# A Fourier mixing layer, a dense Mish layer and their gate: a second-level product more in the dense stage, and y preloaded into PSUM in the last one

## The chip, the cores and the metric

The kernel runs on one core of a Trainium2 chip. The metric is device time in microseconds of one execution of the whole program. Its engines are TensorE (PE: matmuls; PEld: its weight loads), VectorE (DVE), ScalarE (ACT) and GpSimd (POOL); SyncE (SP) issues nearly all DMAs, in one queue. Everything is float32; a matmul takes its operands as `float32r`.

## The reference

```python
x = A_x                                            # 2048 x 640
g = sigmoid((x * gate_w).sum(-1, keepdims=True))
a = einsum("bsd,ed->bse", x, dft_hid_re)
b = einsum("bsd,ed->bse", x, dft_hid_im)
y = einsum("ts,bse->bte", dft_seq_re, a) - einsum("ts,bse->bte", dft_seq_im, b)
h = einsum("bsd,df->bsf", x, w1) + b1              # 640 -> 1728
act = h * tanh(softplus(h))                        # Mish
out = g * y + (1 - g) * einsum("bsf,fd->bsd", act, w2)
```

S = 2048 rows, D = 640 columns, F = 1728 features (13 blocks of 128 and one of 64).

## The kernel before, in words

**Numbers.** Every operand is split in two parts, h (a rounded copy, by ScalarE) and l (the rest, by VectorE): `split`, L127. One product of 128 x 128 by 128 x 512 is `mm3`: three matmuls, high by high, high by low, low by high. A bank of PSUM holds 128 x 512 sums; there are eight, handed out in turn by `psum.get` and `psum.put`.

**Stages.** There are four, one after the other on PE: the transform along the sequence (`seq`, first stored as u), the transform along the hidden axis (`hid`, gives y, stored in `ysc[d][t]`, d for a block of 128 columns, t for a tile of 512 rows), the dense first stage (640 to 1728, with Mish, stored in `asc[f][t]`), and the last stage (`out`, 1728 to 640, with the gate). Each uses the seven-product scheme of Strassen and Winograd over halves: a product of 2 x 2 halves in seven products, with sums of operands ahead and of results behind. The odd fifth block of the 640 columns (the tail) goes along as plain products.

**The dense first stage.** x transposed is the moving operand (`xt[t, k]`, k a block of 128 columns). A pair (fp, tp) takes the features fp and fp + 6 and the tiles t1 = 2 tp and t2 = 2 tp + 1; halves of the columns are blocks 0, 1 and 2, 3. Steps of a pair in `dense_first`: p5 (moving s1), d (the tail d2 for feature fp + 6, a bank of its own), p6 (s2), p3 (s4, with the tail d1), p7 (s3), p2 (a12, the second product A12 B21, with the tail d1), p4 (a22, with the tail d2). The first product, A11 B11, is not there: `dense_quads` (L829) makes it for two features and both tp at once by the seven-product scheme at a second level, in seven steps (a12, a11, s1, s2, s4, s3, a22) of nine matmuls each, for three pairs of features, with banks a and b. Its results go to DRAM (`qout`) and come back as a seed, a copy into the bank a in which the pair's p6, p7 and p4 add on. `dense_rest` computes the last 192 features in steps of 15 and 10 matmuls per tile. `ORDER` puts steps of `dense_rest` (r) and `dense_quads` (q) in turn.

**The last stage.** `ou[0]` computes tiles 0 and 1, `ou[1]` tiles 2 and 3. Order of steps: the first product of `ou[0]` in part, that of `ou[1]`, the rest of the former, then `second` and `third` of each. `second` begins with a `rest` step: the last 192 features for tile t2, in the banks e, e, p4, p4, d2, five matmuls in each. For tiles 2 and 3 act is already multiplied by q = 1 - g (QX in `out_act`, `act_q` for the last 192 features) and y by g (`gate_y`), so they add. For tiles 0 and 1 the results are multiplied by q at the end (`done`, `give`) and the gated y is added (`add_y`).

**Order.** Each engine works its instructions in the order in which the program issues them. The planner runs through the steps; at step i it issues, in this order: operand loads and operand splits (`prep`) of steps up to LEAD or LEAD_D ahead; the step's matmuls; stores that are due; the step's `post` (copies and additions out of its banks); events put there by `at(i, fn)`; then pieces of background jobs (splitting weights, sums of operands, gating of y), for as long as its count of VectorE's time is behind its count of PE's by SLACK, SLACK_D or SLACK_UP, but not in `quiet` steps. `takes`, `spare` and `SPARE` hold back free tiles for later steps. Jobs run in the order of the list `jobs`, not before step `first`.

Of the kernel before, what the change touches and what calls it, by code (L numbers as in the profile page):

```python
# [22 lines left out]
WARM, EARLY = 8, 3  # L23
LEAD = 7
LEAD_D, AHEAD_D = 6, 4
AHEAD = 9
SPARE, SPARE_D, SPARE_OUT = 3, 5, 4
SLACK, SLACK_UP, SLACK_D, QUIET = -1.0, 2.5, 1.0, 2
NR, NFS, NFX, NW, NL = 9, 22, 4, 26, 4
MM = 0.2267  # L30
BACK, NB = 16, 3
NLOAD = 6
QUIET_M, D_END = -1, 24
ORDER, Q_LEAD = "rrqrrqrqrqrqrq", 3
P_LOAD, P_SEED = 8, -1
YG_FIRST, NO_LOAD = 40, 3
XS_FIRST, XS_EACH = 160, 10
R0, R1 = (2, 4), (2, 4)
# [16 lines left out]
def fnet_mish_gate(ctx: ExitStack, tc: tile.TileContext, xn, xt, c_re, c_im, wd_re, wd_im,  # L55
# [28 lines left out]
    def tt(o, a, b, op):  # L84
        clock["dve"] += 0.14 + 0.54 * a.shape[-1] / N
        nc.vector.tensor_tensor(o, a, b, op=op)  # L86
# [4 lines left out]
    def split(h, l, src):  # L91

        copy(h, src)
        tt(l, src, f32(h), OP.subtract)

# [110 lines left out]
    def low(st, k, g, f):  # L206
# [13 lines left out]
        split(*part(st.XA[k], 3 * P, 5 * P), t[:, B2])  # L220
        split(*part(st.XT13[k], 4 * P, 5 * P), t[:, :P])
        split(*t2_part(st, k), t[:, P:2 * P])
# [83 lines left out]
    def add_out(name, f, keep=False):  # L306

        for ps, a in zip(PS[name], f):
            tt(a, ps, a, OP.add)
        if not keep:  # L310
            free_banks(name)
        return f
# [13 lines left out]
    class Problem:  # L326
# [49 lines left out]
        def second(self):  # L376
# [25 lines left out]
            def plus_y(f, d, t):  # L402
                y = YT.pop((d, t))
                tt(f, f, y, OP.add)
                FS.put(y)

            def post(p, k):
# [13 lines left out]
                elif p == "s2":  # L421
                    KEEP["u2"] = add_out("a", ys(t1, 2, 3), True) if self.early else copy_out("a", True)
# [14 lines left out]
            if st.kind == "out":  # L437
# [5 lines left out]
                rest(t2, [("e", 2, True), ("e", 3, True), ("p4", 0, True), ("p4", 1, True), ("d2", 4, True)], e_post)  # L443
            for p, k in in_turn(kh, ("22", "21", "s2", "s1"), ("22", "21", "s2", "s1"), ("22", "21", "s2", "s1")):
# [18 lines left out]
                if k == kh - 1:  # L463
                    takes[i] = (p == "21" or p == "s1" and 2) if self.early else 1 if p == "21" else 2
# [119 lines left out]

        def y_load(self, i, t, *ds):
# [49 lines left out]
    WA, W1, W2C, T2B, QW, extra = [None] * FP, [None] * (FC + 1), {}, [None] * 2, [None] * (FP // 2), []  # L635
# [8 lines left out]
    def quad_job(g, l, m):  # L644
# [3 lines left out]
        WA[2 * g], WA[2 * g + 1], QW[g] = W.get(), W.get(), W.get()  # L648
        split(*WA[2 * g], l)
        split(*WA[2 * g + 1], m)  # L650
        yield 1
        lo, hi = slice(0, P), slice(P, 2 * P)
        for o, u, v in ((0, m[:, lo], l[:, lo]), (1, m[:, hi], m[:, lo]), (2, m[:, hi], t[:, lo]),
                        (3, l[:, hi], t[:, 2 * P:3 * P])):
            tt(t[:, o * P:o * P + P], u, v, OP.subtract)
        FX.put(l, m)
        yield 1
        split(*part(QW[g], 0, 4 * P), t)
        FS.put(t)

    def w1_job(f, ga, gb):
        t = FS.get()
        a, b, c = WA[f], W.get(), W.get()
        if f % KD == 0:
            T2B[f // KD] = W.get()
# [8 lines left out]
        split(*part(b, 0, 2 * P), t[:, B2])  # L674
        split(*part(c, 0, 2 * P), ga[:, A2])
        yield 1
        split(*part(c, 2 * P, 4 * P), gb[:, A2])
        split(*part(c, 4 * P, 5 * P), t[:, :P])
        split(*part(T2B[f // KD], f % KD * P, f % KD * P + P), t[:, P:2 * P])
        FS.put(t)  # L680
        FX.put(ga, gb)
        W1[f] = (a, b, c)
# [23 lines left out]

    def dense_jobs():
        for _ in range(NL):
            jobs.append(Job("lend", simple(lend), w=1))
        def quad(g):  # L710
            jobs.append(Job(("quad", g), lambda l, m: quad_job(g, l, m),
                            lambda: [fx_load(w1a[2 * g + i]) for i in range(2)], 3, 2, 1))
        quad(0)
        jobs.append(Job("w1c", simple(w1c_job), lambda: [fx_load(w1a[FC - 1])], 1, 1))
        jobs.append(Job("w1r", simple(w1r_job), lambda: [fx_load(w1b, KD * FR)], 1, 1))
        quad(1)
        quad(2)
        for f in range(FP):
            jobs.append(Job(("w1", f), lambda a, b, f=f: w1_job(f, a, b),
                            lambda f=f: [fx_load(w1a[f]), fx_load(w1a[f + FP])], 2 + (f % KD == 0), 2))  # L720

    def x_split(key, f):
        r = X[key] = R.get()
        split(r[0], r[1], f)
        FS.put(f)
# [8 lines left out]
    def dense_rest(t, keep, lead, end=False):  # L734
# [9 lines left out]
        def prep(lo, hi):  # L744
            for k in range(lo, hi):
                x_split(keys[k], RAW.pop(("xt", t, k)))
# [6 lines left out]
        def post_c():  # L753
# [3 lines left out]
            store(asc[FC - 1][t], a, a)  # L757
# [8 lines left out]
        def post_r():  # L766
# [7 lines left out]
            def then():  # L774
                nc.scalar.activation(a[q], a[q], AF.Mish)
                store(asc[FC][t], a[q], a)
            at(clock["step"] + 1, then)
            if not keep:
                x_free(*keys)
            else:  # L780
                x_free(*[(names[0], k, t // 2) for k in range(2)])
            if end:
                for w in W1[FC - 1:]:
# [4 lines left out]
        def wait():  # L788
            for key in ("mish", "w1c", "w1r"):
                need(key)  # L790
        step(raw, [wait], mms_c, post_c)
# [7 lines left out]
    XQ = {"a11": xt[0, 0], "a12": xt[0, 1], "a22": xt[2, 1]}  # L799
    XQ.update({o: dr.tile([P, N], F32, name=f"q{o}") for o in ("s1", "s2", "s3", "s4")})  # L800
    XD = {(tp, k, o): dr.tile([P, N], F32, name=f"x{o}_{tp}_{k}") for tp in range(2) for k in range(2) for o in XQ if o[0] == "s"}
    narrow_loads = []
# [495 lines left out]
```

## Time and profile before

| | us |
|---|---|
| three runs | 861.49, 861.83, 862.65 |
| median | 861.83 |
| profiled execution: span, first to last instruction | 860.5 |
| PE busy (3766 matmuls) | 856.2 |
| DVE busy (1281 instructions) | 732.6 |
| ACT busy (903) | 485.6 |
| DMA moved | 233.15 MB, 271 GB/s on the mean |

The page of the profile gives busy times for the whole span; the view by stretches gives them for parts of it, with the clock granted to PE and the share of time in which the DMA engines were busy. The timeline gives instructions one by one: start, length, engine, line, operation, out<-in, count, and in brackets the idle time before it and what ended it. A matmul's 0.39 us overlaps with the next, so the distance from one start to the next is its price. Since all matmuls stand on line 98 and most of DVE's work on line 86, steps are told apart by their place in the order.

### The profile page before, as it was taken

Reading aid. Unit: us, or ns where it says so; the run is one execution under the profiler, and the core shown is the slowest. Engines: PE = TensorE matmul, PEld = TensorE weight load, DVE = VectorE, ACT = ScalarE, POOL = GpSimd, SP = SyncE. Lnnn points to the kernel's source line nnn. Section 1 sums busy time; section 2 is a strip of 40 time slices with the busy share of each in tenths; the row PEclk is TensorE's granted clock in tenths of the full one; section 3 lists DMA queues with packets and bytes.
Section 4 is the critical chain, followed back from the end, with each engine's and each line's share of the span. In section 5 each row is a group of like instructions: output and inputs, shape, how many; then the busy total and the mean of one; then the engine's idle time right before and its main releaser. Section 6 shows DMA issues by size and latency. Waiting matters only on the chain.

```text
span 860.5 us, 12305 instructions
## 1 busy us (share of the span) xinstructions
PE 856.2 (100%) x3766; PEld 708.4 (82%) x3766; DVE 732.6 (85%) x1281; ACT 485.6 (56%) x903; POOL 0.2 (0%) x4
## 2 busy tenths in 40 slices
PE   9999999999999999999999999999999999999998
PEld 8888888888888888888888888888888888888886
DVE  6999988889879789998998897886578979898993
ACT  6756646464555545657656657764646756542442
POOL 0000000000000000000000000000000000000000
PEclk9999999999999999999999999999999999999999
DMA  9975758885768899898676968879998789485952
GB/s 348 345 255 198 252 164 309 281 287 198 255 234 287 280 343 363 274 316 287 207 261 242 319 197 309 287 231 370 357 377 308 230 283 315 152 289 178 353 185 110
DMA packets 126978, 233.15 MB, mean 271 GB/s; under 512 B 14656, under 2 KB 17216, under 8 KB 126912
## 3 DMA queue, kind: packets, MB, share of 16 engines
q1 hardware_dynamic: 126480, 231.72, 77.9%
q8 instruction: 29, 0.48, 0.2%
q10 hardware_dynamic: 432, 0.66, 0.2%
q14 instruction: 37, 0.30, 0.1%
HBM read 180.13 MB, written 52.18 MB: 270 GB/s over the span
## 4 chain that ended last, share of the span: by engine, by line
PE 100%; ACT 0%; issue 0%
PE ps L98 100%; ACT f L89 0%
## 5 line engine op out<-in xcount | busy, mean ns | idle before, releaser
L98 PE MATMUL ps<-rh,wh 128*128 128x512 f32 (+1 forms) x1062 | 412.1, 389 | 0.0
L98 PE MATMUL ps<-rh,wl 128*128 128x512 f32 x1046 | 405.9, 389 | 0.0
L98 PE MATMUL ps<-rl,wh 128*128 128x512 f32 x1045 | 405.9, 389 | 0.0
L89 ACT ACTIVATE rh<-f 128x512 fp32r<-128x512 f32 x419 | 250.8, 626 | 182.7 <-DVE f L86 101.7
L86 DVE TENSOR_TENSOR rl<-f,rh 128x512 fp32r<-128x512 f32 x417 | 272.5, 686 | 41.3 <-ACT rh L89 40.1
L98 PEld LDWEIGHTS ps<-rh,wh 128*128 128x128 f32 x1062 | 199.5, 188 | 41.6 <-DVE f L86 0.3
L98 PEld LDWEIGHTS ps<-rl,wh 128*128 128x128 f32 x1045 | 196.6, 188 | 40.9
L98 PEld LDWEIGHTS ps<-rh,wl 128*128 128x128 f32 x1046 | 196.3, 188 | 40.7
L86 DVE TENSOR_TENSOR f<-f,f 128x512 f32<-128x512 f32 x305 | 208.4, 688 | 9.6 <-DMA f<-act 2.2
L89 ACT ACTIVATE f<-ps 128x512 f32<-128x512 f32 (+1 forms) x145 | 83.2, 596 | 75.2 <-PE ps L98 66.7
L89 ACT ACTIVATE wh<-f 128x512 fp32r<-128x512 f32 (+3 forms) x173 | 76.7, 484 | 46.7 <-DVE f L86 36.5
L86 DVE TENSOR_TENSOR wl<-f,wh 128x512 fp32r<-128x512 f32 (+3 forms) x172 | 82.3, 512 | 20.5 <-ACT wh L89 20.4
L86 DVE TENSOR_TENSOR f<-ps,f 128x512 f32<-128x512 f32 x100 | 65.5, 683 | 16.9 <-PE ps L98 16.7
L98 PE MATMUL ps<-wh,wh 128*128 128x512 f32 x205 | 79.8, 389 | 0.0
L98 PE MATMUL ps<-wl,wh 128*128 128x512 f32 x200 | 77.8, 389 | 0.0
L98 PE MATMUL ps<-wh,wl 128*128 128x512 f32 x199 | 77.4, 389 | 0.0
L98 PEld LDWEIGHTS ps<-wh,wh 128*128 128x128 f32 x205 | 38.5, 188 | 8.2 <-ACT f L89 0.2
L98 PEld LDWEIGHTS ps<-wl,wh 128*128 128x128 f32 x200 | 37.5, 188 | 7.8
L98 PEld LDWEIGHTS ps<-wh,wl 128*128 128x128 f32 x199 | 37.4, 188 | 7.7
L732 ACT ACTIVATE f<-f,b1s 128x512 f32<-128x512 f32 x36 | 25.5, 721 | 31.5 <-DVE f L86 31.5
L86 DVE TENSOR_TENSOR wl<-fx,wh 128x640 fp32r<-128x640 f32 (+3 forms) x50 | 33.7, 680 | 5.9 <-ACT wh L89 5.9
L89 ACT ACTIVATE wh<-fx 128x640 fp32r<-128x640 f32 (+4 forms) x51 | 31.1, 615 | 5.9 <-DMA fx<-in_xn_dram 3.5
(36 smaller groups left out, 176.5 us busy)
## 6 DMA issues: line engine op xcount, KB each, us to landing
f<-in_c_re_dram SPq DMA_DIRECT2D x128, 256.0 KB, 4.0
f<-in_c_im_dram SPq DMA_DIRECT2D x128, 256.0 KB, 4.5
f<-act SPq DMA_DIRECT2D x87, 256.0 KB, 4.9
f<-u SPq DMA_DIRECT2D x80, 256.0 KB, 5.0
act<-f SPq DMA_DIRECT2D x54, 256.0 KB, 5.1
f<-in_xt_dram SPq DMA_DIRECT2D x49, 256.0 KB, 4.6
u<-f SPq DMA_DIRECT2D x40, 256.0 KB, 3.1
y<-f SPq DMA_DIRECT2D x40, 256.0 KB, 4.9
```

The lines of the kernel that those rows point to most:

```text
L86: nc.vector.tensor_tensor(o, a, b, op=op)
L89: nc.scalar.activation(o, a, AF.Copy, scale=scale)
L98: nc.tensor.matmul(ps, a, b, start=start, stop=stop, skip_group_check=True)
L732: nc.scalar.activation(o[rows], src[rows], AF.Mish, bias=b1s[rows, f:f + 1])
```

## The change

Product A12 B21 of the dense first stage, six matmuls a pair plus its tail, leaves `dense_first` and is made in a second call of `dense_quads`, `dense_quads(1)`, between the two calls of `dense_first`. There the banks b start from the first product, A11 B11 (a seed), and the additions bring in the rest of it, so that the sum of both products comes out, with the tail products of d1 among the steps a12, s1, s4 and a22; Mish follows at once for tile t1 (`out_act`). `dense_first` keeps five steps a pair: p5 takes the tail d2 of feature fp + 6 into its bank, and p3 takes the tail of the difference d1 - d2 (`dd`). The step p4 of two pairs is put behind p5 of the next two, and at the very end behind p7. Operand sums for the second call are an added job; weights come in halves, and the tail weights of features 0 to 5 in a job of their own (`five`).

In the last stage, y of tiles 0 and 1 is no longer multiplied by g. `take_y` copies -y into the banks d1 of the first product and e, e, p4, p4, d2 of the `rest` step; two further results have y subtracted. The results are then multiplied by q and y is added, as before: q (b - y) + y. `act_q` goes; its products by q are made in `dense_rest`. The planner's constants and the order of the jobs are new.

```diff
-LEAD_D, AHEAD_D = 6, 4
-AHEAD = 9
-SPARE, SPARE_D, SPARE_OUT = 3, 5, 4
-SLACK, SLACK_UP, SLACK_D, QUIET = -1.0, 2.5, 1.0, 2
+LEAD_D = 6
+AHEAD_D = 6
+AHEAD = 6
+SPARE = 3
+SPARE_D = 2
+SPARE_OUT = 5
+SLACK = -1.0
+SLACK_UP = 2.5
+SLACK_D = 0.0
+QUIET = 2
...
-BACK, NB = 16, 3
+BACK = -17
+NB = 3
...
-QUIET_M, D_END = -1, 24
-ORDER, Q_LEAD = "rrqrrqrqrqrqrq", 3
+QUIET_M = -3
+D_END = 7
+ORDER = 'rrqrrqrrqqrqrqq'
+Q_LEAD = 2
...
+P3_LAG = 2
+Q_LAG = 0
+SEED_Q = 1
...
+JOBS = 'q0 q1 q2 y20 y21 y22 y23 y24 y30 y31 t2 y32 y33 t3 y34 l0 t1 l1 t0 l2 t4 t5 c r l3 l4 l5'
+FIRSTS = {'y20': 37, 'y34': 42, 'l0': 22, 't2': 0}
...
         def first(self, new=False, ks=None):
...
+            if self.out and not (ks and ks[0]):
+                self.take_y("d1", self.t1, 4, len(steps))
...
-                            product(name, b, key, k == 0, last)
+                            product(name, b, key, k == 0 and not (self.out and name == "d1"), last)
...
-                    KEEP["u2"] = add_out("a", ys(t1, 2, 3), True) if self.early else copy_out("a", True)
+                    KEEP["u2"] = add_out("a", ys(t1, 2, 3), True, OP.subtract if self.out else OP.add) if st.kind == "out" else copy_out("a", True)
...
-                rest(t2, [("e", 2, True), ("e", 3, True), ("p4", 0, True), ("p4", 1, True), ("d2", 4, True)], e_post)
+                uses_r = [("e", 2), ("e", 3), ("p4", 0), ("p4", 1), ("d2", 4)]
+                if self.out:
+                    for name, d in uses_r:
+                        self.take_y(name, t2, d, n)
+                rest(t2, [(name, d, not self.out) for name, d in uses_r], e_post)
...
+                self.y_load(n - 2, t1, 0, 1)
+                at(n + 4, lambda: [plus_y(f, j, t1) for j, f in enumerate(KEEP["p1"])])
...
+        def take_y(self, name, t, d, n):
+
+            at(n - 6, lambda: RAW.update({("y", d): fs_load(ysc[d][t])}))
+
+            def put():
+                f, ps = RAW.pop(("y", d)), psum.get()
+                PS.setdefault(name, []).append(ps)
+                copy(ps, f, -1.0)
+                FS.put(f)
+            at(n - 1, put)
...
+    def five_job(f, g):
+        W5[0], T2B[1] = W.get(), W.get()
+        split(*W5[0], f)
+        split(*five_of(KD), g[:, :P])
+        FX.put(f, g)
...
-        split(*WA[2 * g], l)
-        split(*WA[2 * g + 1], m)
+        WA[q, g], QW[q, g] = W.get(), W.get()
+        split(*part(WA[q, g], 0, 4 * P), f)
...
+    def x_diff(key, a, b):
+        f, g = RAW.pop(a), RAW.pop(b)
+        tt(f, f, g, OP.subtract)
+        FS.put(g)
+        x_split(key, f)
...
-    def dense_quads():
+    def dense_quads(q):
...
+        def snap(b, o, more=None):
+            for g, v in enumerate(bank):
                 f = v[o] = FS.get()
                 copy(f, v[b])
+                if q and more:
+                    at(clock["step"] + (o == "q5"), lambda f=f, g=g: plus(f, 2 * g + more[0], more[1]))
+
+        def plus(f, j, tp):
+            c = p1_tile(j, tp)
+            tt(f, f, c, OP.add)
+            FS.put(c)
...
         def out():
             for g, v in enumerate(bank):
-                f = FS.get()
-                copy(f, v["a"])
+                if q:
+                    f = p1_tile(2 * g, 1)
+                    tt(f, v["a"], f, OP.add)
+                else:
+                    f = FS.get()
+                    copy(f, v["a"])
                 save(f, 2 * g, 1)
...
+        def seed():
+            for g, v in enumerate(bank):
+                v["b"] = psum.get()
+                c = p1_tile(2 * g, 0)
+                copy(v["b"], c)
+                FS.put(c)
...
+        for b, x, w, d, post in (("b", "a12", "b21", (0, "d1", 0), lambda: snap("b", "q2")),
+                                 ("a", "a11", "b11", None, lambda: add("a", "q2", 0, 0)),
+                                 ("b", "s1", "t1", (1, "d1", 1), lambda: snap("b", "q5", (1, 1))),
+                                 ("a", "s2", "t2", None, lambda: snap("a", "u2", (1, 0))),
+                                 ("b", "s4", "b22", (1, "de", 0), c12),
+                                 ("a", "s3", "t3", None, lambda: add("a", "q5", 1, 1)),
+                                 ("a", "a22", "t4", (0, "d1", 1), out)):
...
                     mm3(v[b], *block(g, w), *X["xq", x], start, True)
+                    if q and d:
+                        mm3(v[b], *five_of(2 * g + d[0]), *X[d[1], 0, d[2]], False, True)
...
+                if q:
+                    at(n - SEED_Q, seed)
+                    p1_loads(n - P_Q_0, 0, 0)
...
-                ([lambda: need(("w1", fp))], sub(fp, [("b", "s1", at_cols(2, 0), True, True)]), p5_post),
-                ([], sub(fp, [], [("d", "d2", 1, True, True)]), d_post),
-                ([], sub(fp, [("a", "s2", t2_at(fp), False, True)]), p6_post),
-                ([], sub(fp, [("b", "s4", at_cols(1, 2 * P), False, False)], [("b", "d1", 1, False, True)]), p3_post),
-                ([], sub(fp, [("a", "s3", at_cols(2, 2 * P), False, True)]), p7_post),
-                ([], sub(fp, [("c", "a12", at_cols(0, 2 * P), True, False)], [("c", "d1", 0, False, True)]), p2_post),
-                ([], sub(fp, [("a", "a22", at_cols(1, 0), False, False)], [("a", "d2", 0, False, True)]), p4_post)]
+                ([lambda: need(("w1", fp))], sub(fp, [("b", "s1", at_cols(1, 0), True)], [("b", "d2", 1)]), p5_post),
+                ([], sub(fp, [("a", "s2", t2_at(fp), False)]), p6_post),
+                ([], sub(fp, [("b", "s4", at_cols(0, 2 * P), False)], [("b", "dd", 1)]), p3_post),
+                ([], sub(fp, [("a", "s3", at_cols(1, 2 * P), False)]), p7_post),
+                ([], sub(fp, [("a", "a22", at_cols(0, 0), False)], [("a", "d2", 0)]), p4_post)]
...
+            p5, p6, p3, p7, p4 = zip(parts(fp), parts(fp + 1))
+            for two in (p5, late_p4, p6, p3, p7) + ((p4,) if end and fp == FP - 2 else ()):
                 for p in two:
                     step([], *p)
...
+            late_p4[:] = p4
...
-    yg_jobs(0, 1)
-    aq_jobs()
-    yg_jobs(2, 3)
...
-    dense_first(0, False, [("s1", n0 + 2), ("s2", n0 + 7), ("s4", n0 + 9), ("s3", n0 + 11)], quads)
+    dense_first(0, False, [("s1", n0 + T0[0]), ("s2", n0 + T0[1]), ("s4", n0 + T0[2]), ("dd", n0 + T0[3]), ("s3", n0 + T0[4])])
+    nq = len(steps)
+    for _ in dense_quads(1):
+        pass
     n0 = len(steps)
```

More of the change, by code (lines that the diff above doesn't have):

```diff
@@ L84, in tt @@
     def tt(o, a, b, op):
-        clock["dve"] += 0.14 + 0.54 * a.shape[-1] / N
+        n = 1
+        for m in a.shape[1:]:
+            n *= m
+        clock["dve"] += 0.14 + 0.54 * n / N
         nc.vector.tensor_tensor(o, a, b, op=op)
@@ L94, in split, with splits @@
         tt(l, src, f32(h), OP.subtract)
+    def splits(*hls):
+        for h, l, src in hls:
+            copy(h, src)
+        for h, l, src in hls:
+            tt(l, src, f32(h), OP.subtract)
     def mm(ps, a, b, start, stop):
@@ L756, in post_c, with then @@
             psum.put(ps)
-            store(asc[FC - 1][t], a, a)
+            def then():
+                tt(a, a, QT[t], OP.mult)
+                store(asc[FC - 1][t], a, a)
+            if t < 2:
+                return store(asc[FC - 1][t], a, a)
+            at(clock["step"] + 1, then)
         def mms_r():
@@ L914, in mms @@
             def mms():
-                a, b, c = W1[fp]
-                for bank, name, blk, start, stop in ops:
+                b, c = W1[fp]
+                for bank, name, blk, start in ops:
                     if start:
@@ L944, in seed @@
             H["a", f] = psum.get()
-            copy(H["a", f], KEEP["p1", f])
+            p1 = KEEP.pop(("p1", f))
+            copy(H["a", f], p1)
+            FS.put(p1)
         def pop(bank, fp):
@@ L1163, in fnet_mish_gate @@
     rests = [r for r in rests for _ in range(2)]
-    quads = dense_quads()
+    quads = dense_quads(0)
     for o in ORDER:
@@ L1184, in fnet_mish_gate @@
         ou[tp].third()
-    late = {id(asc[c][t]): ("aq", t) for c in (FC - 1, FC) for t in (2, 3)}
     for n, prep in attach:
```

321 lines of the change are left out of this document (182 added, 139 removed).

## The prediction

> **What bounds the kernel now.** I read the page first, then the chain that ended last, then the busy time by stretches. Columns of the stretches: the stretch, then busy time and instruction count of PE, PEld, DVE, ACT and POOL, the granted clock, the DMA share and GB/s. The four stretches are the sequence transform, the hidden transform, the dense first stage and the last stage.
>
> ```profile
> span 860.5 us, 12305 instructions
> PE 856.2 (100%) x3766; PEld 708.4 (82%) x3766; DVE 732.6 (85%) x1281; ACT 485.6 (56%) x903; POOL 0.2 (0%) x4
> ...
> PE 100%; ACT 0%; issue 0%
> ```
>
> ```profile
> 0.77 856.26 PE ps L98 x3766
> 857.03 0.02 issue
> 857.05 0.60 ACT f L89
> ```
>
> ```profile
> 0.00:394.00 394.00, 393.23 (x1725) 325.63 (x1726) 347.29 (x600) 218.16 (x394) 0.20 (x4) 1.00 0.81 276
> 394.00:518.00 124.00, 124.00 (x549) 102.67 (x548) 111.77 (x197) 81.40 (x156) 0.00 (x0) 1.00 0.75 258
> 518.00:686.00 168.00, 168.00 (x742) 138.78 (x741) 128.62 (x245) 106.31 (x210) 0.00 (x0) 1.00 0.88 310
> 686.00:857.00 171.00, 171.00 (x755) 141.28 (x753) 144.97 (x241) 79.18 (x145) 0.00 (x0) 1.00 0.67 233
> ```
>
> The chain is one unbroken run of 3766 matmuls, 0.77 to 857.03 us, at clock 1.00. In the dense stretch 742 matmuls take 168 us, 0.2264 us each. The starts say the same more exactly (timeline of PE and DVE near the end of the dense stage):
>
> ```profile
> 677.56 0.39 PE L98 MATMUL ps<-rh,wl 128*128 128x512 f32 x1
> 677.79 0.39 PE L98 MATMUL ps<-rh,wh 128*128 128x512 f32 x1
> ...
> 678.92 0.39 PE L98 MATMUL ps<-rh,wl 128*128 128x512 f32 x1
> 679.15 0.39 PE L98 MATMUL ps<-wh,wh 128*128 128x512 f32 x1
> ...
> 682.15 0.69 DVE L86 TENSOR_TENSOR f<-ps,f 128x512 f32<-128x512 f32 x1
> ```
>
> From 677.56 to 679.15 there are seven starts, 0.227 us each. So time is the number of matmuls times 0.227 us, plus any wait of PE; now there is practically no wait. Each matmul removed is worth 0.227 us, and each wait added costs its full length.
>
> **The change, part by part: matmuls.** One step of `mm3` is three matmuls. Before, a pair (fp, tp) issues in `dense_first` p5 6, d 3, p6 6, p3 9, p7 6, p2 9 and p4 9 = 48; twelve pairs give 576, `dense_quads` gives 7 x 3 x 3 = 63: 639. After, a pair issues p5 9 (the d2 tail is now in its bank), p6 6, p3 9, p7 6, p4 9 = 39, so 468; the two calls of `dense_quads` give 63 each, and the second also carries four tails x 3 groups x 3 = 36: 630. The last stage has the same products, with only the start flag changed. So 9 matmuls go of 3766: 9 x 0.227 = 2.04 us. That is all the gain there is. No PE idleness is left to win, and start and tail of the program are untouched.
>
> **VectorE, ScalarE and DMA: hidden as totals.** Durations by shape:
>
> ```profile
> L86 DVE TENSOR_TENSOR rl<-f,rh 128x512 fp32r<-128x512 f32 x417 | 272.5, 686 | 41.3 <-ACT rh L89 40.1
> L89 ACT ACTIVATE rh<-f 128x512 fp32r<-128x512 f32 x416 | 249.1, 626 | 182.0 <-DVE f L86 101.7 <-PE ps L98 65.6 <-DMA f<-in_c_re_dram 2.5
> L86 DVE TENSOR_TENSOR f<-f,f 128x512 f32<-128x512 f32 x303 | 207.2, 688 | 9.6 <-DMA f<-act 2.2 <-DMA xs<-f 1.1 <-DMA out_dram<-f 0.8
> L89 ACT ACTIVATE f<-ps 128x512 f32<-128x512 f32 x141 | 80.8, 596 | 70.2 <-PE ps L98 61.7 <-DVE rl L86 2.0 <-issue 1.4
> L86 DVE TENSOR_TENSOR f<-ps,f 128x512 f32<-128x512 f32 x100 | 65.5, 683 | 16.9 <-PE ps L98 16.7
> L86 DVE TENSOR_TENSOR wl<-fx,wh 128x640 fp32r<-128x640 f32 x28 | 22.7, 819 | 2.1 <-ACT wh L89 2.1
> L89 ACT ACTIVATE ps<-f 128x512 f32<-128x512 f32 x40 | 22.7, 593 | 12.7 <-DVE f L86 12.7
> ```
>
> VectorE loses 24 bank additions (d and p2, 0.683 each: 16.4 us) and ten gate products of y (0.688: 6.9). It gains 18 additions in the second quads (12.3), nine operand splits net (0.686: 6.2), three tail differences (2.1), four sums for the second set of moving operands (2.8) and four subtractions of y in the last stage (2.7). Weight splitting moves from full rows to halves: three jobs of two 0.819 and one 0.686, about 7.0 us without their small differences, become six jobs of two 0.686 and one job of 0.819, about 9.1; the small differences and the 128-wide rest cost under 2 us more. Net about +6 us on 732.6, some 2 of them in the dense stretch, whose 128.6 of 168 us leave room. ScalarE gains nine copies for splits (0.626), nine snapshots (0.596), and three seeds and six y preloads (0.593), about 16 us, plus some in weights, on 485.6. In DMA the ten gated stores of y and the traffic of `act_q` (four loads, four stores, two loads of q moved) go; twelve more loads and some stores of the first product's tiles, the second set's sums and ten more loads of xt come: a dozen transfers more in a dense stretch busy at 0.88. On totals no second engine becomes the bound, and I cost all this at nothing. If that cover failed, the 6 us of VectorE would stand on the path.
>
> **Where PE must now wait: order.** The price of a late hand-over stands in the trace of before once:
>
> ```profile
> 573.55 0.68 DVE L86 TENSOR_TENSOR f<-ps,f 128x512 f32<-128x512 f32 x1
> ```
>
> ```profile
> 574.29 0.19 PEld L98 LDWEIGHTS ps<-rh,wh 128*128 128x128 f32 x1 [0.30 <-DVE f L86]
> ```
>
> That is p7's addition from bank a, and p4 waiting to write on: PE's weight load starts 0.06 us after the addition ends. Unhindered, a weight load starts together with the matmul before its own:
>
> ```profile
> 602.53 0.39 PE L98 MATMUL ps<-rl,wh 128*128 128x512 f32 x1
> 602.54 0.19 PEld L98 LDWEIGHTS ps<-rh,wl 128*128 128x128 f32 x1
> 602.76 0.39 PE L98 MATMUL ps<-rh,wl 128*128 128x512 f32 x1
> ```
>
> The other end, an engine that waits for the matmul (timeline of PE, DVE, ACT):
>
> ```profile
> 637.44 0.39 PE L98 MATMUL ps<-wh,wl 128*128 128x512 f32 x1
> ...
> 637.87 0.69 DVE L86 TENSOR_TENSOR f<-ps,f 128x512 f32<-128x512 f32 x1 [0.78 <-PE ps L98]
> ```
>
> ```profile
> 856.63 0.39 PE L98 MATMUL ps<-wh,wl 128*128 128x512 f32 x1
> ...
> 857.05 0.60 ACT L89 ACTIVATE f<-ps 128x512 f32<-128x512 f32 x1 [0.76 <-PE ps L98]
> ```
>
> So a bank is read 0.42 to 0.43 us after its last matmul starts, at best.
>
> *The preload of y.* `take_y` fills the five banks of the rest step of `ou[0].second` with -y in the events of the step before. In that step events come behind the step's post, which copies banks a (KEEP["p1"]) on the same ScalarE. The program before has these two steps and copies, without the preloads:
>
> ```profile
> 710.88 0.39 PE L98 MATMUL ps<-rh,wl 128*128 128x512 f32 x1
> ...
> 711.56 0.39 PE L98 MATMUL ps<-rh,wl 128*128 128x512 f32 x1
> 711.79 0.39 PE L98 MATMUL ps<-rh,wh 128*128 128x512 f32 x1
> ```
>
> ```profile
> 711.54 1.66 ACT L89 ACTIVATE wh<-f 128x512 fp32r<-128x512 f32 x3
> 713.10 1.06 ACT L89 ACTIVATE f<-ps 128x512 f32<-128x512 f32 x2
> ```
>
> 710.88 is the last matmul on the second bank a, 711.56 the last of the step, 711.79 the first on e. With an idle ScalarE the second copy starts at 710.88 + 0.42 = 711.30. Two copies take 1.06, so one follows another by 0.46: the first preload starts at 711.76, ends at 712.35, and PE loads at 712.41. Unhindered that load is at the last matmul of the step, 711.57: wait 0.84 us, the lower end. With ScalarE as late as it was here (the copies began at 713.10, behind weight splits), the preload starts at 714.02, ends at 714.61, load at 714.67: 3.10 us, the upper end. The other four preloads follow at 0.46, faster than PE's five matmuls a bank (1.13), so the first alone counts. I take 1.1, nearer the lower end: before most bank copies ScalarE was idle and waiting for PE (61.7 of 70.2 us of idleness there), so lateness is the rarer state. The preload of d1 for `first` has the last p4 steps before it, and I take 0 for it.
>
> *Bank hand-backs by VectorE.* In the quads s3 and a22 now stand next to each other: six matmuls (1.36 us) between the last on a bank and the first of the next product, which must wait for the addition. So the addition may start at most 1.36 - 0.68 - 0.06 = 0.62 us after that matmul; 0.43 is the least. At the end of the dense stage p4 of the last pair follows p7 directly, again with six between. Before, twelve to 24 stood there. How late VectorE was:
>
> ```profile
> 552.89 0.39 PE L98 MATMUL ps<-rh,wl 128*128 128x512 f32 x1
> ...
> 554.59 1.87 DVE L86 TENSOR_TENSOR f<-ps,f 128x512 f32<-128x512 f32 x3
> ```
>
> s3: 554.59 - 552.89 = 1.70 us late, so 1.08 of wait in either quads. p7 of the last pair: 682.15 - 677.56 = 4.59, so 3.97 of wait. The least lag gives 0 each. Which it will be depends on what the planner puts ahead on VectorE, and there SLACK_D falls from 1.0 to 0.0 and the order of jobs is new; I take 0, and keep 0 to 1.08 and 0 to 3.97 for the range. The seeds of the second quads (ScalarE, one step ahead) need nothing of the step they stand in: 0.
>
> **The sum.** Against the profiled execution: span 860.5 - 2.04 + 1.1 = 859.6. The median shown, 861.83, lies 1.33 above that span; the same 1.33 gives **860.9 us**, 0.1% under the time before. About 0.2%, 1.72 us, is what can be told from no change here: faster ends at 860.1, slower begins at 863.55.
>
> **Rivals.** *No wait at all:* the preload is hidden and the full 2.04 shows: 859.8. For it: PE of before runs without gaps with many such hand-overs. Against it: copies and preload stand on one queue in that order. *VectorE late at the last pair:* p7 at its old lag adds 3.97 and one s3 1.08: 861.83 - 2.04 + 1.1 + 3.97 + 1.08 = 865.9, slower. With 1.1 at the preload it decides from a lag of 3.3 us (863.55 - 860.9 + 0.62) at that p7. For it: the old lag of 4.59, and weight jobs still to run there. Against it: the order of those jobs is new, and such a job needs weight slots that the last pair still holds. *ScalarE late at the preload:* the 3.10 of its upper end: 862.9, still within 0.2%. *The removed matmuls buy nothing:* if PE had slack, the time would stay at 861.8 with the 1.1 in it; the even starts speak against it. The Trainium skill, page Trace Analysis, section Identifying the Most-Contended Engine, holds matmul busy time for no good measure and goes by the busy share of weight loads, 82% here, which would leave PE 18% of headroom and the nine matmuls worth little; the trace disagrees as far as this stream goes, since its starts never leave 0.227 us. On a single wait of 4 us the skill's page TensorE: Matmul & The Clock Gate (section HAM oscillation) adds that idleness over about 3.4 us lets the clock fall; before shows only clock 1.00, so no run tells yet.
>
> **Chances.** Forecast, with waits between 0.3 and 3.7 us in all: 0.50, range of its own 860.1 to 863.5 (the late preload within it). No wait or almost none: 0.24. VectorE late, slower: 0.24. Nothing bought: 0.02, within 0.2%. So faster 0.24, same 0.52, slower 0.24. Range: low 859.6, just under the full gain; high 864.6, into the late case up to 3.7 of wait beyond the forecast.
>
> **What would show it.** Matmuls: 3757, and the dense stage 2 us shorter in matmuls. The preload: PE weight load on a bank e waiting for ACT, 0.8 to 3.1 us, 108 matmuls or 24.5 us into the last stage. VectorE: weight loads waiting for DVE at a22 and at the last p4. Totals: DVE near 739 us, ACT near 503. Wrong would be: PE without any such wait at the preload, waits above 1 us at another place, a pitch other than 0.227, or a DMA as releaser.

## The result, and the profile after

| | before | after |
|---|---|---|
| median of 14 runs each, us | 861.77 (861.49 to 862.68) | 863.88 (863.18 to 864.77) |
| ratio after / before | | 1.0023 (95% interval 1.0015 to 1.0031) |
| span of the profiled execution | 860.5 | 862.2 |
| matmuls | 3766 | 3757 |

The change made the kernel slower by 0.23%. The page of the changed kernel, its busy times and then the shares of the chain that ended last:

```profile
span 862.2 us, 12400 instructions
PE 855.5 (99%) x3757; PEld 706.1 (82%) x3757; DVE 739.1 (86%) x1296; ACT 501.6 (58%) x933; POOL 0.2 (0%) x4
...
PE 94%; DVE 2%; ACT 2%; DMA 1%; issue 1%; SPq 0%; DVEq 0%
```

Nine matmuls are gone, as counted, and DVE and ACT have grown to about the totals that were worked out (739 and 503). But the chain is no longer PE alone. In order of time (start, length, what):

```profile
0.77 525.11 PE ps L141 x2307
...
554.11 5.37 DMA p<-f
559.54 2.76 DMA f<-p
...
567.20 108.24 PE ps L141 x476
...
683.75 28.21 PE ps L141 x123
712.47 0.60 ACT ps L125
713.12 145.37 PE ps L141 x640
```

Up to 525.9 us and from 567.2 us on PE leads, with breaks ahead of 683.75 and 713.12. Between, the chain follows ScalarE, VectorE and transfers for 41 us of the dense stage, though PE itself stands still for only 2.6 of them. The stretches (PE, PEld, DVE, ACT, POOL, clock, DMA share, GB/s) say where matmuls are missing:

```profile
394.00:518.00 124.00, 124.00 (x549) 102.67 (x548) 114.78 (x203) 83.23 (x158) 0.00 (x0) 1.00 0.78 261
518.00:686.00 168.00, 166.33 (x729) 136.21 (x728) 129.42 (x249) 118.10 (x231) 0.00 (x0) 1.00 0.89 311
686.00:858.00 172.00, 171.50 (x757) 141.71 (x756) 148.40 (x249) 81.88 (x153) 0.00 (x0) 1.00 0.72 248
```

The hidden stage runs 549 matmuls in its 124 us, as before. In the 168 us of the dense stage there are 729 in place of 742. The loss can be read from the starts of all matmuls, behind the first 7 us, where they stand 0.43 us apart in both kernels. What their distances have above 0.2267 us is the wait; the 0.1 us by which the matmul right behind a wait is late is counted with it. The whole loss lies in five places:

| wait ahead of | at, us | us | what is late |
|---|---|---|---|
| a22, first quads | 555.17 | 0.99 | VectorE's addition from the bank of s3 |
| second p6 | 562.98 | 0.35 | the seed: first product through DRAM |
| first p3 (its tail) | 566.47 | 1.22 | split of the tail difference dd |
| p4 of the last pair | 683.75 | 0.42 | VectorE's addition from the bank of p7 |
| rest step, last stage | 713.12 | 0.76 | preload of -y by ScalarE |
| sum | | 3.74 | |

In the kernel before the same search finds 0.15 us. The waits added, 3.74 - 0.15, less the 2.04 of the nine matmuls make 1.55 us; from the 41st matmul to the last one the time grew from 844.56 to 846.24 us, by 1.68, so about 0.1 is left unexplained. The spans differ by 1.7 as well, but they hold the start, which varies: in the fourteen traces of this case the 41st matmul starts between 11.10 and 12.22 us. The waits that the trace names for PE's weight loads (line waited for: us in total, times, longest; the first has 0.42 us from the start of the program, at 4.64 us):

```profile
PEld ps L141 <- ACT wh L125: 2.4, 3, 1.1
...
PEld ps L141 <- ACT ps L125: 1.4, 2, 0.9
...
PEld ps L141 <- DVE f L122: 0.6, 1, 0.6
PEld ps L141 <- DVE wl L122: 0.5, 1, 0.5
```

One name here misleads. The timeline at a22:

```profile
552.67 0.39 PE L141 MATMUL ps<-rh,wl 128*128 128x512 f32 x1
...
554.03 0.39 PE L141 MATMUL ps<-rh,wl 128*128 128x512 f32 x1
...
554.35 1.87 DVE L122 TENSOR_TENSOR f<-ps,f 128x512 f32<-128x512 f32 x3
554.53 1.14 ACT L125 ACTIVATE wh<-f 128x512 fp32r<-128x512 f32 x2
```

```profile
555.14 0.19 PEld L141 LDWEIGHTS ps<-wh,wh 128*128 128x128 f32 x1 [1.14 <-ACT wh L125]
```

552.67 is s3's last matmul on its first bank. The addition from that bank starts 1.68 us later and, at 0.68 us, ends at 555.03; PE's load follows at 555.14. A copy on ScalarE, the first of the two at 554.53, ends at nearly the same moment and gets the name, but it is a split for a later step: in the run with banks of its own for a22, below, the same copy starts only when a22 is under way. The next two waits (queue of SP, then ACT, PEld, DVE):

```profile
554.11 1.94 SPq L1367 DMA_DIRECT2D p<-f  x3
559.54 0.32 SPq L195 DMA_DIRECT2D f<-p  x1
```

```profile
562.32 0.60 ACT L125 ACTIVATE ps<-f 128x512 f32<-128x512 f32 x1 [1.36 <-DMA f<-p]
...
565.78 0.63 ACT L125 ACTIVATE wh<-f 128x512 fp32r<-128x512 f32 x1 [1.23 <-DVE f L122]
```

```profile
562.98 0.19 PEld L141 LDWEIGHTS ps<-wh,wh 128*128 128x128 f32 x1 [0.50 <-ACT ps L125]
566.47 0.19 PEld L141 LDWEIGHTS ps<-wh,wh 128*128 128x128 f32 x1 [0.88 <-ACT wh L125]
```

```profile
563.29 0.43 DVE L122 TENSOR_TENSOR wl<-fx,wh 128x256 fp32r<-128x256 f32 x1 [1.20 <-ACT wh L125]
...
565.07 0.69 DVE L122 TENSOR_TENSOR f<-f,f 128x512 f32<-128x512 f32 x1
```

The first product of feature 1 leaves for DRAM at 554.11. Its load is issued only at 559.54, when the store has landed (5.37 us in the chain above), and lands 2.76 us later; the seed waits on ScalarE until 562.32, idle for 1.36 us. Weight splits behind it come late (DVE idle for 1.20 at 563.29), the tail difference at 565.07 stands behind those, and p3 waits for its split. At the last p4, and at the rest step:

```profile
681.84 0.39 PE L141 MATMUL ps<-wh,wl 128*128 128x512 f32 x1
...
683.01 0.68 DVE L122 TENSOR_TENSOR f<-ps,f 128x512 f32<-128x512 f32 x1
```

```profile
683.74 0.19 PEld L141 LDWEIGHTS ps<-rh,wh 128*128 128x128 f32 x1 [0.58 <-DVE f L122]
713.12 0.19 PEld L141 LDWEIGHTS ps<-rh,wh 128*128 128x128 f32 x1 [0.92 <-ACT ps L125]
```

```profile
711.35 1.22 ACT L125 ACTIVATE f<-ps 128x512 f32<-128x512 f32 x2 [0.18 <-PE ps L141]
...
712.47 1.63 ACT L125 ACTIVATE ps<-f 128x512 f32<-128x512 f32 x3
```

p7's addition starts 1.17 us after the bank's last matmul and ends at 683.69. At the rest step ScalarE, not late at all, copies the two banks a and then preloads: 712.47 + 0.60 = 713.07, and PE loads at 713.12.

### The profile page after: what moved, and what is told of

Same layout as the page of the kernel before. It is cut to its first block, busy times and chain, and to the rows that moved or that the text cites. A ratio compares the mean times of both kernels' runs of the same rounds, so it can differ in the third digit from the quotient of the medians.

```text
span 862.2 us, 12400 instructions
## 1 busy us (share of the span) xinstructions
PE 855.5 (99%) x3757; PEld 706.1 (82%) x3757; DVE 739.1 (86%) x1296; ACT 501.6 (58%) x933; POOL 0.2 (0%) x4
## 4 chain that ended last, share of the span: by engine, by line
PE 94%; DVE 2%; ACT 2%; DMA 1%; issue 1%; SPq 0%; DVEq 0%
PE ps L141 94%; DVE f L122 1%; ACT f L125 1%; ACT wh L125 1%; DMA p<-f 1%; DVE rl L122 1%; DVE wl L122 1%; DMA act<-f 0%; DMA f<-p 0%; ACT rh L125 0%; ACT f L831 0%; DVE f L874 0%; DVE fx L122 0%; ACT ps L125 0%; ACT f L879 0%
## 5 line engine op out<-in xcount | busy, mean ns | idle before, releaser
L125 ACT ACTIVATE rh<-f 128x512 fp32r<-128x512 f32 (+1 forms) x427 | 256.0, 626 | 181.4 <-DVE f L122 87.7
L122 DVE TENSOR_TENSOR rl<-f,rh 128x512 fp32r<-128x512 f32 x425 | 277.8, 685 | 52.7 <-ACT rh L125 45.6
L122 DVE TENSOR_TENSOR f<-f,f 128x512 f32<-128x512 f32 (+1 forms) x337 | 225.3, 674 | 9.1 <-ACT f L125 1.3
L125 ACT ACTIVATE f<-ps 128x512 f32<-128x512 f32 (+1 forms) x153 | 88.6, 594 | 73.8 <-PE ps L141 68.4
L125 ACT ACTIVATE wh<-f 128x512 fp32r<-128x512 f32 (+3 forms) x188 | 85.3, 495 | 52.4 <-DVE f L122 49.2
L122 DVE TENSOR_TENSOR wl<-f,wh 128x512 fp32r<-128x512 f32 (+3 forms) x188 | 92.7, 526 | 20.5 <-ACT wh L125 20.1
L141 PE MATMUL ps<-wl,wh 128*128 128x512 f32 x192 | 74.8, 390 | 0.2 <-DVE wl L122 0.2
L122 DVE TENSOR_TENSOR f<-ps,f 128x512 f32<-128x512 f32 x83 | 53.8, 681 | 13.3 <-PE ps L141 13.2
L125 ACT ACTIVATE ps<-f 128x512 f32<-128x512 f32 x49 | 27.7, 594 | 17.7 <-DVE f L122 12.9
L122 DVE TENSOR_TENSOR wl<-fx,wh 128x640 fp32r<-128x640 f32 (+4 forms) x44 | 28.5, 654 | 6.6 <-ACT wh L125 6.6
```

The lines of the kernel that those rows point to most:

```text
L125: nc.scalar.activation(o, a, AF.Copy, scale=scale)
L141: nc.tensor.matmul(ps, a, b, start=start, stop=stop, skip_group_check=True)
```

## The experiments

All start from the changed kernel. Waits are read from matmul starts as above, in us, and belong to the one execution that was profiled; times are medians of all executions, in brackets that of the kernel before, run next to it on the same chip, to which the ratios in the text refer. The two can lie apart: the profiled execution of the step between s3 and a22 took 867.98 us against a median of 865.67, that of the three fixes 860.86 against 861.82. The first runs each move or undo one part of the change, the later ones put such edits together. p6 is the second p6 of the first two pairs; in "four, own banks" 1.4 of the 2.1 stand ahead of the first one. In the three rows with 4.0 and 4.2 at the first p3, some 1.3 to 1.7 us are not waiting but matmuls at a lower clock (last section).

| run | a22 | p6 | first p3 | last p4 | rest | elsewhere | sum | time (before) |
|---|---|---|---|---|---|---|---|---|
| after | 0.99 | 0.35 | 1.22 | 0.42 | 0.76 | | 3.7 | 863.88 (861.77) |
| preload two steps ahead | 0.82 | 0.10 | 1.23 | 0.43 | 0 | | 2.6 | 863.08 (861.96) |
| first product kept | 1.09 | 0 | 0.10 | 0.44 | 0.77 | | 2.4 | 862.53 (861.96) |
| step between s3 and a22 | 0 | 2.4 | 4.0 | 0.44 | 0.77 | | 7.5 | 865.67 (861.96) |
| all four | 0 | 1.2 | 4.0 | 0 | 1.04 | | 6.2 | 864.91 (861.96) |
| own banks for a22 | 0 | 1.87 | 1.53 | 0.43 | 0.77 | 0.42 | 5.1 | 865.20 (862.09) |
| no jobs at the end | 1.43 | 0.16 | 1.23 | 0 | 1.94 | | 4.8 | 865.40 (862.09) |
| four, own banks | 0 | 2.1 | 4.2 | 0 | 0 | | 6.3 | 866.59 (862.09) |
| three fixes | 0.82 | 0 | 0.42 | 0 | 0 | | 1.25 | 861.82 (862.09) |
| three, quiet ahead of s3 | 0.40 | 0 | 1.56 | 0 | 0 | 0.42 | 2.4 | 862.89 (862.16) |
| three, tail earlier | 0.99 | 0 | 0 | 0 | 0 | | 1.0 | 861.35 (862.16) |
| three, both | 0.44 | 0 | 0 | 0 | 0 | 1.81 | 2.3 | 862.84 (862.16) |
| tail earlier, bias later | 0.58 | 0 | 0 | 0 | 0 | 0.37 | 1.0 | 861.57 (861.87) |

A difference of a few tenths at one place in one trace is not yet an effect of an edit. Six of these kernels (after, the preload two steps ahead, first product kept, no jobs at the end, three fixes, three with the tail earlier) issue the same instructions on PE, VectorE and ScalarE up to a22, and a22 waits between 0.82 and 1.43 us in them.

**The preload, two steps ahead.**

```diff
-            at(n - 1, put)
+            at(n - 2, put)
```

> The copies of -y into the banks stand two steps ahead of their product and not one. Theory (the wait of 0.76 us at the rest step of tile 1 comes from two bank copies ahead of the first preload on ScalarE's queue): that wait is gone, the other four stay, 863.1 us, 0.8 under the changed kernel's 863.9. Rival (ScalarE as a whole is late there, with its copies for operands): the wait stays at 0.4 us or more, or comes back within the next two steps, and the time stays within 0.3 us of 863.9.

The wait at the rest step is gone. Those at p3 and the last p4 stay; the 0.17 and 0.25 us less at a22 and p6 stand over 100 us ahead of the first instruction that the edit moves and are no effect of it. The time fell by 0.80 us, ratio to before 1.0011 (1.0003 to 1.0020). The order on ScalarE's queue was the cause.

**The first product kept.**

```diff
+            elif j < 2 and not tp:
+                KEEP["p1", j] = f
+                store(qout[j][tp], f, None, 1)
             else:
                 store(qout[j][tp], f, f, 1)
...
-                if True:
+                if tp or fp:
```

(A store with None for its tile leaves the tile to the seed.)

> The first product of features 0 and 1 for the first two tiles stays in its tile in SBUF for the seed, as in the kernel before, and is stored besides for the second quads. Theory (the seed waits for a trip through DRAM, and with it everything behind it on ScalarE, the split of the tail difference too): both the wait of 0.35 us at the second p6 and that of 1.22 us at the first p3 are gone, 862.3 us, 1.6 under 863.9. Rival (the split of the tail difference is late on VectorE by itself): only the 0.35 us go, 863.5 us.

Both waits go, down to 0.10, so the theory holds and the rival falls: the late tail difference was a consequence of the seed's trip through DRAM. That it went by the queue of ScalarE and then that of VectorE is read from the rows above. Time 1.35 us less, ratio 1.0005 (0.9996 to 1.0014).

**A step between s3 and a22.**

```diff
-ORDER = 'rrqrrqrrqqrqrqq'
+ORDER = 'rrqrrqrrqqrqqrq'
```

> A step of ten matmuls of the last 192 features is put between s3 and a22 of the first quads. Theory (a22 waits for VectorE's addition from the bank on which s3 ended; with 16 matmuls between in place of six there are 3.6 us for it): the wait of 0.99 us at a22 is gone, the others stay within 0.3 us of what they were, 862.9 us. Rival (the operand of a22 is late on ScalarE, as the trace names it): ten matmuls, 2.3 us, would hide that too; but then its split ends later than the matmul before it. If all engines are late as a whole there, the wait comes back elsewhere within 10 us and the time stays at 863.9.

The wait at a22 goes, but the second seed and the tail difference come later by more: 865.67 us, ratio 1.0052 (1.0039 to 1.0065). It doesn't tell bank from operand, and the forecast of the time was wrong; the last case of the expectation came, a wait that comes back elsewhere, and more came back than had gone. Three rows of ScalarE show where, the first from the changed kernel, the others from this run:

```profile
552.42 0.60 ACT L125 ACTIVATE f<-ps 64x512 f32<-64x512 f32 x1 [1.06 <-PE ps L141]
```

```profile
554.81 0.60 ACT L125 ACTIVATE f<-ps 64x512 f32<-64x512 f32 x1 [3.59 <-PE ps L141]
...
563.71 0.60 ACT L125 ACTIVATE ps<-f 128x512 f32<-128x512 f32 x1 [1.44 <-DMA f<-p]
```

The copy out of the moved step now lets ScalarE stand idle for 3.59 us in place of 1.06, with everything behind it in the queue. And the seed's load, issued at 559.10, lands only 4.6 us later, in place of 2.8: six stores of the first product now leave in a row ahead of it, where there were three. Which of the two made the tail difference late is not shown.

**All four together** (with no jobs started in the last steps of the dense stage, below).

> All four together: preload two steps ahead, first product kept in SBUF, the step between s3 and a22, and no background jobs started in the last eight steps but two of the dense stage. Theory (five waits, 3.74 us, are all that stands between 9 matmuls fewer and the measured time): PE without a wait above 0.2 us, 863.9 - 3.7 = 860.2 us, below the kernel before (861.8) by 0.19%. Rival (the dense stretch as a whole lacks time on VectorE or ScalarE): waits reappear elsewhere, more than 1.5 us of them, and it stays above 861.5 us.

864.91 us, ratio 1.0035 (1.0022 to 1.0047): here the rival was right. The same copy on ScalarE stood idle again, and the name in the row misleads once more:

```profile
554.68 0.60 ACT L125 ACTIVATE f<-ps 64x512 f32<-64x512 f32 x1 [3.18 <-DMA act<-f]
```

```profile
553.84 0.39 PE L141 MATMUL ps<-rl,wh 128*128 128x512 f32 x1
```

553.84 is the last matmul of the moved step, and a bank is read 0.42 us behind that at best, at 554.26. So most of the 3.18 us went to waiting for PE, and only the last 0.4 to the tile that a store was still reading. The seed is in its tile here, but its copy stands behind this one in the queue, and the first pair paid.

**Banks of its own for a22.** The order of steps stays; only the dependence on s3's addition goes.

```diff
+        def s3_out():
+            if not q:
+                snap("a", "k")
+            add("a", "q5", 1, 1)
+            if not q:
+                free("a")
...
-                                 ("a", "a22", "t4", (0, "d1", 1), out)):
+                                 ("a" if q else "c", "a22", "t4", (0, "d1", 1), out)):
```

> In the first quads a22 goes to banks of its own; the sum so far is copied out of banks a by ScalarE behind s3 and added to it at the end, so a22 needs nothing of the additions behind s3. Order of steps as in the changed kernel. Theory (bank hand-back: a22 waits for VectorE's addition from the bank on which s3 ended): the wait of 0.99 us ahead of a22 goes, 862.9 us, if the three additions more do not delay the second seed. Rival (the operand split on ScalarE, which the trace names as the releaser): the wait stays at 0.9 us or more, 863.9 us. Three more additions on VectorE (1.9 us) may lengthen the two waits behind it by up to that much.

The wait at a22 is gone, and two rows of this run rule out the split that the trace named:

```profile
554.50 0.39 PE L141 MATMUL ps<-wh,wh 128*128 128x512 f32 x1
```

```profile
555.72 1.14 ACT L125 ACTIVATE wh<-f 128x512 fp32r<-128x512 f32 x2
```

a22 starts at 554.50; the split, at the same place in ScalarE's order, starts 1.2 us after it. So it was the bank, not the operand. But 865.20 us, ratio 1.0037 (1.0025 to 1.0049): with the three additions, copies and tiles more the second p6 starts at 563.76 in place of 562.98 and the first p3's tail at 567.54 in place of 566.47, and PE, now a microsecond earlier, waits the longer for them. The waits at the two grew by 1.8 us together.

**No jobs at the end of the dense stage.**

```diff
     n_dense = len(steps)
+    quiet |= set(range(n_dense - 8, n_dense - 2))
```

> No background jobs are started in the last eight steps but two of the dense stage; nothing else changes. Theory (VectorE is late at the last p7 because of weight splitting ahead of its addition): the wait of 0.42 us at the last p4 goes, 863.4 us. Rival (it is late with its own additions and products by q): the wait stays at 0.3 us or more. The weight splitting moves into the last stage, where it may make the preload's wait of 0.76 us longer, by up to 1 us.

The wait at the last p4 goes, so weight splitting had made VectorE late there. The splits land in the first steps of the last stage, where ScalarE is now late for the preload: 1.94 in place of 0.76 us. Two rows of ScalarE in this run show it:

```profile
711.67 0.61 ACT L125 ACTIVATE wh<-f 128x512 fp32r<-128x512 f32 x1
712.19 1.06 ACT L125 ACTIVATE f<-ps 128x512 f32<-128x512 f32 x2
```

The copies of banks a begin at 712.19, behind a split, and no longer as soon as PE is done. 865.40 us, ratio 1.0038 (1.0025 to 1.0050). From the 41st matmul on its profiled execution is 0.98 us longer than that of the changed kernel, which is what its waits give (4.8 for 3.7); that execution, 864.67 us, was the fastest of five, and why the others took longer is not shown.

**Four fixes, three fixes.** The first has the preload two steps ahead, the first product kept, the quiet end and the banks for a22; the second leaves the banks out.

> Preload two steps ahead, first product kept in SBUF, a22 in banks of its own, no jobs at the end of the dense stage. Theory (five separate waits): at most 0.4 us of waits left, 860.3 us, 0.17% under the kernel before. Rival (the stretch around the first quads lacks time as a whole): over 1.5 us of waits, above 861.5 us.

> The same without banks of its own for a22. Theory: of the waits only that ahead of a22 is left (1.0 to 1.1 us) with 0.1 us at the tail difference, 861.0 us, about 0.1% under the kernel before. Rival as for the four: above 861.9 us.

Four: 866.59 us, ratio 1.0047 (1.0035 to 1.0060), the rival's case. Its ScalarE has this row:

```profile
558.15 0.60 ACT L125 ACTIVATE f<-ps 128x512 f32<-128x512 f32 x1 [3.40 <-DMA actr<-f]
```

A snapshot waits 3.40 us for a tile whose store has not ended: five tiles more are held at once, and ScalarE's queue stands still for them. Three: 861.82 us, ratio 0.9997 (0.9988 to 1.0006), about the time before and 0.8 us over what was expected. What is left is a22 (0.82) and the tail difference (0.42, expected 0.1).

**The last two waits.** No jobs in the two steps ahead of s3 and a22 (QUIET_M back to -1); the tail difference a step earlier (T0 of dd 7 for 8); both; and the addition of the bias in the step ahead of s3 put behind s3's additions:

```diff
-            nc.vector.scalar_tensor_tensor(a[q], ps[q], b1s[q, FC:], b[q], op0=OP.add, op1=OP.add)
-            psum.put(ps)
-            FS.put(b)
+            def bias():
+                nc.vector.scalar_tensor_tensor(a[q], ps[q], b1s[q, FC:], b[q], op0=OP.add, op1=OP.add)
+                psum.put(ps)
+                FS.put(b)
+            later(int(end), bias)
```

> The three fixes, and no background jobs in the two steps ahead of s3 and a22 of the first quads (QUIET_M -1 as before the change). Theory (VectorE's addition behind s3 is late by what is queued ahead of it): the piece of weight splitting ahead of it (0.47 us) leaves, the wait of 0.8 us at a22 falls to 0.3 to 0.4; what then stays is the addition with the bias ahead of it, which itself waits for the step of ten matmuls. Time 861.4 us. Rival (the weights that are put off are needed 10 us later): the gain comes back as a wait at a p5 or p6 of the first pair.

> The three fixes, and the tail difference for p3 made one step earlier (T0 of dd 7 for 8). Theory (it stands on VectorE behind a piece of weight splitting that itself waits for ScalarE): the wait of 0.42 us at the first p3 goes, that at a22 stays at 0.8 us, 861.4 us. Rival (the piece then delays another operand): it reappears within ten steps.

> Both of these. Theory: 0.3 to 0.4 us of waits left in all, 861.0 us, 0.1% under the kernel before, with its profile's matmuls ending 1.6 us earlier. Rival: as for the two.

> The version with the tail difference earlier, and in the last step of ten matmuls ahead of s3 the addition of the bias on VectorE (0.73 us) goes behind s3's additions in place of ahead of them; its Mish comes a step later. Theory (a22 waits for an addition that is late by what VectorE's queue holds ahead of it): the additions start up to 0.7 us earlier, the wait of 0.99 us at a22 falls to 0.3 to 0.6 us, PE has no other, 860.8 us, 0.15% under the kernel before. Rival (what bounds it is the addition's own wait for matmuls or ScalarE): the wait at a22 stays at 0.9 us or more, 861.35 us.

Quiet ahead of s3: a22 waits 0.40, as expected, and the weights put off cost 1.56 at p3 and 0.42 at the second p7: the rival, only a few steps later than it said, 862.89 us, 1.0008 (1.0000 to 1.0017). Tail earlier: its wait is gone and nothing came back, 861.35 us, 0.9992 (0.9983 to 1.0001). Both: 862.84 us, 1.0007 (0.9999 to 1.0016), forecast 861.0 and wrong: 1.81 us come back at the second p7, where the weight load waits for a copy of ScalarE behind weight splits. Bias later: a22 waits 0.58 for 0.99, as expected; VectorE in that run:

```profile
552.88 0.56 DVE L122 TENSOR_TENSOR wl<-fx,wh 128x384 fp32r<-128x384 f32 x1 [0.67 <-ACT wh L125]
553.36 1.88 DVE L122 TENSOR_TENSOR f<-ps,f 128x512 f32<-128x512 f32 x3
555.15 0.73 DVE L876 SCALAR_TENSOR_TENSOR f<-ps,b1s,f 64x512 f32<-64x512 f32 x1
```

The additions now stand ahead of the bias; what still delays them is a piece of weight splitting that waits for ScalarE. A bank handed back later by ScalarE, at the second p7 again, cost 0.37 of it, and the forecast of the time, 860.8, was missed: 861.57 us, 0.9997 (0.9988 to 1.0006). The best version is the one with the tail earlier; in the middle of its runs it lies 0.08% under the kernel before, with an interval that still touches no difference. A version without any wait was not found.

## Why the prediction was wrong

The forecast was 860.9 us, no change that can be told; measured were 863.88, 2.1 us over the time before. The range held it; the case that came, slower, was the one forecast at 0.24. All waits together were taken at 1.1 us and came to 3.74: the preload 0.76 for 1.1, the bank hand-backs 1.41 and the way through DRAM 1.57, both taken at nothing.

*Nine matmuls, 2.04 us:* right. 3757 matmuls, and waits and gain add up to within 0.1 us. In the best version the weight loads have one wait left behind the start, 1.15 us at a22 (the other 0.25 of the first line are at 4.48 us):

```profile
PEld ps L141 <- ACT wh L125: 1.4, 2, 1.1
PEld ps L141 <- issue: 0.7, 1, 0.7
```

With 1.0 us of waits it takes 843.30 us from the 41st matmul to the last one, 1.26 less than before, where 2.04 less the 0.85 of waits more would be 1.2. So the removed matmuls did pay. The Trainium skill (Perfetto Trace Analysis, Identifying the Most-Contended Engine) judges TensorE's headroom by FLOPs and by the busy share of weight loads. That share is 82% before and after; on this stream, with starts 0.2267 us apart, the other 18% was no headroom that could be used.

*The preload, 1.1 us from 0.84 to 3.10:* the mechanism was right, the size lay below the lower end at 0.76. ScalarE was not late, so the term was 0.34 too large. A late ScalarE occurs too: the run without jobs at the end had 1.94. Part of the miss is in how such a wait was priced, by the delay of the weight load. That came out nearly as forecast, 713.12 - 712.23 = 0.89 us; but a matmul that was held up starts together with its own load (both at 713.12), and not 0.23 us behind it, and the next one loses 0.11. So the time lost is about 0.1 less than the load's delay, at a22 and the last p4 too.

*Bank hand-backs by VectorE, taken at 0:* this is the first step that failed. The price stood in the prediction (1.08 for s3, up to 3.97 at the last p7), and the old lag of s3 was nearly the new one: 1.70 and 1.68 us, worth 0.99. At the last p7 the lag fell from 4.59 to 1.17 and cost 0.42. Taking for s3 the value of the nearest row, not the free end, would have given 1.1 more; for the last p7 that row would have been far too high.

*"On totals no second engine becomes the bound, and I cost all this at nothing":* the second step that failed, and the dearest. The totals were right, but the first product of features 0 and 1 went through DRAM where before it stayed in its tile, and it was needed some 10 us after it was made, of which the way through DRAM took 8.2 (554.11 to 562.30). The kernel of the change shows that; the sum counted the transfers and not when they land. Two of the prediction's own signs of being wrong came with it: a wait above 1 us at another place (1.22 at p3), and a transfer as what is waited for. With what queued behind it, it cost 0.35 + 1.22 = 1.57 us. Without this one term the result was 862.5, as the run with the first product kept shows, which can't be told from no change. The forecast would have been met in that, though not in its mechanism: 2.4 us of waits, and more than half of them VectorE's bank hand-backs taken at 0.

*The seeds of the second quads and the preload of d1, taken at 0:* right, no wait there.

*The rivals:* the slower one came true in its kind, VectorE late at bank hand-backs, but at a22 more than at the last p7, and not alone. "No wait at all" was not reached by any of the twelve runs.

## What to carry to other kernels

Where one engine runs without a gap, an edit that removes its work is worth little unless every hand-over that it moves closer is checked: distance in matmuls against the other engine's lag, taken from the old trace at the same place. A tile that goes through memory is priced by the time from its making to its use, and by everything queued behind the instruction that waits for it. A mended wait often pays into the next one; here quiet steps and banks of its own cost time, tiles or cover elsewhere, so the sum of all waits is to be read after each edit.

## What the hardware showed

After two waits of PE close together its clock was lower for some 3 us, in three of the fourteen traces. In the run with a step between s3 and a22 (stretches: PE, PEld, DVE, ACT, POOL, clock, DMA share, GB/s):

```profile
563.00:566.00 3.00, 1.64 (x7) 1.38 (x8) 1.32 (x5) 2.23 (x6) 0.00 (x0) 1.00 0.87 337
566.00:569.00 3.00, 1.42 (x8) 0.84 (x6) 2.24 (x7) 0.72 (x2) 0.00 (x0) 1.00 0.49 159
569.00:571.00 2.00, 1.77 (x4) 1.26 (x5) 1.90 (x6) 2.00 (x7) 0.00 (x0) 0.66 0.00 0
571.00:573.00 2.00, 2.00 (x6) 1.52 (x6) 0.83 (x3) 1.32 (x3) 0.00 (x0) 0.50 0.74 206
```

After waits of 2.4 and 1.7 us with 2.6 us of matmuls between, and 0.5 more one matmul later, the granted clock was 0.50 from about 570 to 573 us and matmuls started 0.43 us apart, some 1.7 us more on top of the waits. The other two are the runs with all four edits and with four fixes. What decides is open: waits of 1.9 and 1.5 us, as close, left the clock at 1.00 in the trace of the run with banks of its own for a22. The Trainium skill (TensorE: Matmul & The Clock Gate, HAM oscillation) tells of idle gaps above about 3.4 us; here neither wait was that long. In the changed kernel itself, with waits of 1.22 us at most, the clock stayed at 1.00.
